# Bias generator without GpSimd and with 19 evict buffers; second unit's loads behind the bias writes

## The chip, the cores and the metric

The kernel runs on one core of one Trainium2 chip. The metric is the device time of one execution in microseconds, median over several runs; lower is better. Times in the profile are in microseconds from the start of the span.

## What is computed

Attention with a learned relative bias, followed by a two-matrix feed-forward block; 4 batches, 8 heads, sequence 576, head width 64, feed-forward 512 to 2048 to 512:

```python
scores = scale * np.matmul(q, k.transpose(0, 1, 3, 2))
psi_rel = np.log1p(np.abs(pos[:, None] - pos[None, :]))
psi_i = np.log1p(np.maximum(pos[:, None], 1.0))
h = np.maximum((psi_rel / psi_i)[..., None] @ w1 + b1, 0.0)   # 32 hidden units
scores = scores + (h @ w2).transpose(2, 0, 1)[None]           # bias of 8 heads
attn = softmax(scores)
x = np.matmul(attn, v)          # to (tokens, 512)
h = x @ w_in
out = np.maximum(0.01 * h, h) @ w_out
```

The bias depends on the position of the row and on the distance alone, and is the same for all four batches.

## The kernel before, in words

The work has three stages on the same engines. The **generator** makes the bias rows and writes them to a scratch buffer in device memory; **attention** works through 16 units (4 pairs of heads by 4 batches) of 9 tiles; then the **feed-forward** block runs in token blocks of 512.

**The generator** takes 36 row groups T of 16 rows each, in the order of the list GEN. For one group the relu rows r (128 partitions: 4 rows by 32 hidden units; up to 576 columns) are made four times: by VectorE (DVE) or GpSimd (POOL) with an add and a max (L111), or by ScalarE (ACT) as a Relu (L109). A planner at L87 to L97 picks the engine: it keeps a running load for each and gives each relu to the one that would be done first. Its costs for a row of w columns are 0.24 + 0.00072 w us on ACT, 0.11 + 0.00056 w on DVE and 0.2 + 0.0044 w on POOL, with 0.84 us on ACT per group for the evictions. Its plan gives 18 relus to ACT, 114 to DVE and 12 to POOL. Rows r come from a ring of 13 buffers. TensorE multiplies the four with w2 (L122), ACT copies the result from PSUM in two pieces into an evict buffer e (L129, L130; a ring of 5), and SyncE's queue (SP) writes e to the scratch buffer scr (L141, 295.5 KB). `gen_tick(g)` writes this down in the order: relus of group g+1 (and of g+3 on POOL), matmuls of g, eviction of g-1. `load_bias` loads finished parts of scr into bias tiles, named 0, 1, M, 2, 3, three loads each (two for M); the ticks at which this is done stand in a table in `gen_tick`.

**Attention.** All generator ticks are written ahead of the first attention tile (GEN_AT). A unit u needs its q and k, loaded by `load_unit` (four loads of 288 and 304 KB, L177 and L178) into one of two sets of buffers raw, and v, by `load_v` (three loads). q and k are then split into a rounded part and a rest: `split_hi` is a cast on DVE (L193 for q, L198 for k), `split_lo` a subtraction on POOL (L205 for q, L208 for k, in two pieces). The 9 tiles of a unit are A0 B0 A1 B1 M A2 B2 A3 B3; tile n belongs to unit n // 9. `step(n)` writes the scores of tile n (L231, first with the rounded k, then with its rest), bias and minimum on DVE (L253), the exponential on ACT (L254), then the reciprocals of the tile before, the product with v (PV, L331) where one is due, and the transposes (L291) of tile n-3. The table SPL says behind which tile of a unit the next unit's splits stand; at tile 4 `load_unit(u+2)`, at tile 8 `load_v(u+2)` is written. Bias tiles A2, B2 use part 2, and A3, B3 part 3.

**What sets the order.** Every engine runs its own list in the order in which the code writes it, SP as well: one queue issues all DMAs, and an issue that waits holds back all issues behind it. The 8 DMA semaphores go round, so that an issue also waits for the landing of the one eight places ahead of it.

Attention output goes to tiles xs for the first 512 tokens and to x1 (four tiles of 128 by 1792) for the rest. x1 is empty until the first unit's output.

## Time and profile before

| | us |
|---|---|
| runs | 746.71, 748.47, 748.63 (median 748.47) |
| the profiled execution's own time | 747.11 |
| its span | 745.3 |
| generator: first relu to first L253 of attention | 4.17 to 61.28 |
| unit 0 (tiles 0 to 8) | 61.28 to 72.38 |
| unit 1 (tiles 9 to 17) | 72.38 to 90.60 |
| units 2, 3, 4 | 16.6, 16.5, 16.5 each |
| busy PE, DVE, ACT, POOL | 717.7, 400.0, 367.2, 151.3 |

A tile's start is the start of its L253. Busy PE counts pipelined matmuls whose ends are modelled, so 96% of the span isn't a TensorE at its peak. DVE and POOL are busiest in the generator, whose relus are theirs.

### The profile page before, as it was taken

Reading aid. Unit: us, or ns where it says so; the run is one execution under the profiler, and the core shown is the slowest. Engines: PE = TensorE matmul, PEld = TensorE weight load, DVE = VectorE, ACT = ScalarE, POOL = GpSimd, SP = SyncE. Lnnn points to the kernel's source line nnn. Section 1 sums busy time; section 2 is a strip of 40 time slices with the busy share of each in tenths; the row PEclk is TensorE's granted clock in tenths of the full one; section 3 lists DMA queues with packets and bytes.
Section 4 is the critical chain, followed back from the end, with each engine's and each line's share of the span. In section 5 each row is a group of like instructions: output and inputs, shape, how many; then the busy total and the mean of one; then the engine's idle time right before and its main releaser. Section 6 shows DMA issues by size and latency. Waiting matters only on the chain.

```text
span 745.3 us, 11450 instructions
## 1 busy us (share of the span) xinstructions
PE 717.7 (96%) x4192; PEld 555.9 (75%) x4192; DVE 400.0 (54%) x1011; ACT 367.2 (49%) x797; POOL 151.3 (20%) x179
## 2 busy tenths in 40 slices
PE   6899999999999999998999999999999999999998
PEld 3236787777777777876887888888888888888896
DVE  8998778778788888848999311111211221111211
ACT  4778677876777777774555321222212222112221
POOL 2684444444354444400000000000000000000000
PEclk9999999999999999999999999999999999999999
DMA  9889839733936653102553010000100000000100
GB/s 222 260 241 263 205 86 234 162 83 112 262 88 165 164 165 91 37 22 78 177 172 110 1 56 1 1 0 1 57 0 1 0 27 31 0 1 1 57 1 29
DMA packets 30264, 68.27 MB, mean 92 GB/s; under 512 B 8192, under 2 KB 8320, under 8 KB 30208
## 3 DMA queue, kind: packets, MB, share of 16 engines
q1 hardware_dynamic: 30208, 67.54, 32.9%
q8 instruction: 33, 0.54, 0.3%
q14 instruction: 23, 0.19, 0.1%
HBM read 51.92 MB, written 15.61 MB: 91 GB/s over the span
## 4 chain that ended last, share of the span: by engine, by line
PE 80%; DVE 9%; ACT 6%; DMA 3%; issue 1%; POOL 0%; DVEq 0%; POOLq 0%; ACTq 0%
PE ps_o L435 13%; PE ps_t L435 13%; PE ps_o L331 10%; PE ps_s L461 9%; PE ps_s L462 9%; PE ps_s L463 9%; PE ps_s L231 6%; PE ps_t L291 6%; DVE p L253 3%; ACT p L254 3%; DVE r L111 3%; ACT PT L307 2%; PE ps_t L122 1%; PE ps_o L122 1%; PE ps_s L122 1%
## 5 line engine op out<-in xcount | busy, mean ns | idle before, releaser
L450 DVE TENSOR_TENSOR gl<-g,gh 128x512 fp32r<-128x512 f32 (+1 forms) x80 | 51.0, 638 | 270.5 <-ACT g L444 270.5
L231 PE MATMUL ps_s<-ks,qs 128*128 128x288 f32 x640 | 119.5, 313 | 1.5 <-DVE mx L253 1.5
L254 ACT ACTIVATE p<-p,mx 128x576 f32<-128x576 f32 x128 | 99.5, 777 | 38.3 <-DVE mx L253 21.4
L461 PE MATMUL ps_s<-woh,gh 128*128 128x512 f32 x288 | 113.7, 395 | 1.6 <-ACT g L444 1.6
L462 PE MATMUL ps_s<-wol,gh 128*128 128x512 f32 x288 | 113.9, 395 | 0.0
L463 PE MATMUL ps_s<-woh,gl 128*128 128x512 f32 x288 | 113.0, 392 | 0.5 <-DVE gl L450 0.5
L253 DVE CUSTOM_DVE_ANT_0 p<-ps_s,bias 128x576 f32<-128x576 f32 x128 | 95.0, 752 | 29.8 <-PE ps_s L231 26.8
L231 PEld LDWEIGHTS ps_s<-ks,qs 128*128 128x128 f32 x640 | 89.6, 189 | 2.9 <-DVE mx L253 2.2
L307 ACT COPY PT<-ps_t 128x512 f32<-128x512 f32 x128 | 73.4, 574 | 30.1 <-PE ps_t L291 29.9
L443 ACT ACTIVATE gh<-ps_o 128x512 fp32r<-128x512 f32 (+1 forms) x39 | 21.5, 552 | 127.8 <-PE ps_o L435 127.8
L291 PE MATMUL ps_t<-ident,p 128*128 128x128 f32 x512 | 79.5, 278 | 3.4 <-ACT PT L307 2.5
L443 ACT ACTIVATE gh<-ps_t 128x512 fp32r<-128x512 f32 (+1 forms) x39 | 21.5, 551 | 114.4 <-PE ps_t L435 114.2
L291 PEld LDWEIGHTS ps_t<-ident,p 128*128 128x128 f32 x512 | 58.5, 140 | 21.1 <-ACT PT L307 7.5
L331 PE MATMUL ps_o<-PT,v 128*64 128x288 f32 x512 | 69.2, 412 | 0.4 <-ACT PT L298 0.4
L461 PEld LDWEIGHTS ps_s<-woh,gh 128*128 128x128 f32 x288 | 54.2, 188 | 14.3 <-ACT g L444 2.0
L463 PEld LDWEIGHTS ps_s<-woh,gl 128*128 128x128 f32 x288 | 54.4, 189 | 13.6 <-DVE gl L450 1.3
L462 PEld LDWEIGHTS ps_s<-wol,gh 128*128 128x128 f32 x288 | 54.3, 189 | 11.6
L435 PE MATMUL ps_o<-xh,wil 128*128 128x512 f32 (+1 forms) x156 | 58.5, 375 | 0.0
L435 PE MATMUL ps_o<-xl,wih 128*128 128x512 f32 (+1 forms) x156 | 58.4, 375 | 0.0
L435 PE MATMUL ps_t<-xh,wil 128*128 128x512 f32 (+1 forms) x156 | 58.3, 374 | 0.0
L435 PE MATMUL ps_o<-xh,wih 128*128 128x512 f32 (+1 forms) x156 | 58.2, 373 | 0.0
L435 PE MATMUL ps_t<-xl,wih 128*128 128x512 f32 (+1 forms) x156 | 58.1, 373 | 0.0
(93 smaller groups left out, 1133.2 us busy)
## 6 DMA issues: line engine op xcount, KB each, us to landing
raw<-kt SPq DMA_DIRECT2D x32, 304.0 KB, 7.3
scr<-e SPq DMA_DIRECT2D x32, 295.5 KB, 3.4
raw<-qt SPq DMA_DIRECT2D x32, 288.0 KB, 7.0
raw<-wi SPq DMA_DIRECT2D x16, 512.0 KB, 3.8
raw<-wo SPq DMA_DIRECT2D x16, 512.0 KB, 3.6
bias<-scr SPq DMA_DIRECT2D x16, 288.0 KB, 4.1
out<-x SPq DMA_DIRECT2D x18, 256.0 KB, 2.1
v<-vm SPq DMA_DIRECT2D x16, 256.0 KB, 6.2
```

The costliest lines, as they stand in the source:

```text
L231: nc.tensor.matmul(s_[:, S0 + HS * hh:S0 + HS * hh + HS], qs[:, c0:c0 + 128], ks[:, k0 + HS * hh:k0 + HS * hh + HS], start=(j == 0), stop= ...
L253: nc.vector.tensor_tensor_reduce(out=p, in0=s_[:, S0:S0 + S], in1=bt, scale=-0.125, scalar=3.4e38, op0=ALU.add, op1=ALU.min, accum_out=i)
L254: nc.scalar.activation(out=p, in_=p, func=AF.Exp, bias=i, scale=-1.0, accum_out=sm_t[n][:, col:col + 1])
L291: nc.tensor.transpose(t0[:, 128 * jb:128 * jb + 128], p[:, p0 + 128 * jb:p0 + 128 * jb + 128], ident[:])
L307: nc.scalar.copy(out=PT[u, g][:, 0:8, c].rearrange("p (j h) c -> p j h c", h=2)[:, :, h, :], in_=t0[:].rearrange("p (j c) -> p j c", j=4))
L331: nc.tensor.matmul(o[64 * h:64 * h + 64, 0:HS], l, r, start=(jb == 0), stop=(jb == 4))
L435: nc.tensor.matmul(h_[:, :N], w, x[:, :N], start=(j == 0), stop=(j == len(mms) - 1))
L443: nc.scalar.activation(out=gh[:, :N], in_=h_[:, :N], func=AF.Prelu, alpha=0.01)
L450: nc.vector.tensor_sub(gl[:, :N], g[:, :N], gh[:, :N].bitcast(F32))
L461: nc.tensor.matmul(o, gh[:, c], wt[m][2][:], start=(m == 0), stop=False)
L462: nc.tensor.matmul(o, gh[:, c], wt[m][3][:], start=False, stop=False)
L463: nc.tensor.matmul(o, gl[:, c], wt[m][2][:], start=False, stop=(m == MF - 1))
```

## The change

The evict buffers become 19: seven tiles of their own, and twelve pieces of 591 columns in the four x1 tiles, taken in turn. The planner loses POOL: all relus go to ACT (22) and DVE (122). The ring of rows r shrinks from 13 to 9. The ticks at which bias parts are loaded move, and part 3 leaves the table. `load_unit(1)` and `load_v(1)` move from the start of the program to behind the generator, with the load of bias part 3 between them. A table SPL0 puts unit 1's splits behind tiles 5 to 8 of unit 0 (SPL: tiles 0 to 7), and unit 2's q and k loads are written at tile 8 of unit 0 (tile 4 before).

```diff
@@ -26,6 +26,7 @@
 GEN = [16, 17] + list(range(16)) + [34, 35] + list(range(18, 26)) + list(range(33, 25, -1))
 SPL = {0: [(0, "q")], 1: [(1, "q", 0)], 3: [(1, "q", 1)], 4: [(0, "k")], 5: [(1, "k", 0)], 7: [(1, "k", 1)]}
 GEN_AT = [39] * 9
+SPL0 = {5: [(0, "q")], 6: [(1, "q", 0), (1, "q", 1)], 7: [(0, "k")], 8: [(1, "k", 0), (1, "k", 1)]}
 LAG = 3
 BLK = 512
 BLOCKS = [(BLK * i, min(BLK, NT - BLK * i)) for i in range((NT + BLK - 1) // BLK)]
@@ -65,6 +66,9 @@
     cs = gp.tile([128, S + 214], F32, name="cs")
     bps = gp.tile([128, 144], F32, name="bps")
     warm = gp.tile([128, 1], F32, name="warm")
+    W = S + 15
+    e_b = [gp.tile([128, W], F32, name=f"e{i}")[:] for i in range(7)]
+    e_b += [x1[h][:, W * i:W * i + W] for h in range(HP) for i in range(3)]
     psib, ips, ltw = cs[:, 34:178], cs[:, 178:214], cs[:, 214:214 + S]
     w1c, b1c, w2d = cs[:, 0:1], cs[:, 1:2], cs[:, 2:34]
 
@@ -84,31 +88,29 @@
     def gen_w(T):
         return max(S - 16 * T, 16 * T + 16)
 
-    plan, load = [], {"a": 0.0, "v": 0.0, "p": 15.0}
+    plan, load = [], {"a": 0.0, "v": 0.0}
     for T in GEN:
         w = gen_w(T)
         load["a"] += 0.84
-        cost = {"a": 0.24 + 0.00072 * w, "v": 0.11 + 0.00056 * w, "p": 0.2 + 0.0044 * w}
+        cost = {"a": 0.24 + 0.00072 * w, "v": 0.11 + 0.00056 * w}
         eng = ""
         for _ in range(4):
-            e = min((c for c in cost if c != "p" or "p" not in eng and len(plan) >= 2), key=lambda c: load[c] + cost[c])
+            e = min(cost, key=lambda c: load[c] + cost[c])
             load[e] += cost[e]
             eng += e
-        plan.append("".join(sorted(eng, key="avp".index)))
-
-    def gen_r(g, pool):
+        plan.append("".join(sorted(eng)))
+
+    def gen_r(g):
         T = GEN[g]
         w = gen_w(T)
-        r = gr.setdefault(T, [None] * 4)
+        r = gr[T] = [None] * 4
         for q, c in enumerate(plan[g]):
-            if (c == "p") != pool:
-                continue
             k = 4 * T + q
-            t = gp.tile([128, S], F32, tag="r", name="r", bufs=13)
+            t = gp.tile([128, S], F32, tag="r", name="r", bufs=9)
             if c == "a":
                 nc.scalar.activation(out=t[:, :w], in_=ltw[:, :w], func=AF.Relu, bias=bps[:, k:k + 1])
             else:
-                (nc.gpsimd if pool else nc.vector).tensor_scalar(out=t[:, :w], in0=ltw[:, :w], scalar1=bps[:, k:k + 1], scalar2=0.0, op0=ALU.add, op1=ALU.max)
+                nc.vector.tensor_scalar(out=t[:, :w], in0=ltw[:, :w], scalar1=bps[:, k:k + 1], scalar2=0.0, op0=ALU.add, op1=ALU.max)
             r[q] = t
 
     def gen_mm(T):
@@ -125,8 +127,8 @@
     def gen_ev(T):
         pt, o0 = gps.pop(T)
         R, F = 16 * T + 15, S - 16 * T
-        e = gp.tile([128, S + 15], F32, tag="e", name="e", bufs=5)
-        nc.scalar.activation(out=e[:, R:], in_=pt[:, o0:o0 + F], func=AF.Copy, scale=ips[:, T:T + 1])
+        e = e_b[GEN.index(T) % len(e_b)]
+        nc.scalar.activation(out=e[:, R:W], in_=pt[:, o0:o0 + F], func=AF.Copy, scale=ips[:, T:T + 1])
         nc.scalar.activation(out=e[:, 0:R], in_=pt[:, o0 + R:o0:-1], func=AF.Copy, scale=ips[:, T:T + 1])
         if T < 16:
             c, r0 = str(T // 8), 16 * (T % 8)
@@ -137,19 +139,17 @@
         else:
             c, r0 = "M", 32 + 16 * (T - 34)
         a = r0 * H * PIT + 1
-        dst = scr[c][a:a + 16 * (H * PIT + 1)].rearrange("(i x) -> i x", i=16)[:, 0:H * PIT].rearrange("i (h p) -> i h p", h=H)[:, :, 0:S + 15]
-        nc.sync.dma_start(out=dst, in_=e[:])
+        dst = scr[c][a:a + 16 * (H * PIT + 1)].rearrange("(i x) -> i x", i=16)[:, 0:H * PIT].rearrange("i (h p) -> i h p", h=H)[:, :, 0:W]
+        nc.sync.dma_start(out=dst, in_=e)
 
     def gen_tick(g):
         if g + 1 < 36:
-            gen_r(g + 1, False)
-        if g + 3 < 36:
-            gen_r(g + 3, True)
+            gen_r(g + 1)
         if 0 <= g < 36:
             gen_mm(GEN[g])
         if 0 <= g - 1 < 36:
             gen_ev(GEN[g - 1])
-        for c in {13: "0", 28: "1", 31: "M", 38: "23"}.get(g, ()):
+        for c in {16: "0", 24: "1", 26: "M", 34: "2"}.get(g, ()):
             load_bias(0, c)
 
     bias = {}
@@ -472,9 +472,8 @@
 
     with tc.manual_schedule():
         gen_setup()
-        for u in range(2):
-            load_unit(u)
-            load_v(u)
+        load_unit(0)
+        load_v(0)
         sp_ops = [(u, w, a) for u in range(1) for w, a in (("q", None), ("q", 0), ("q", 1), ("k", None), ("k", 0), ("k", 1))]
         done = -1
         early_ops = []
@@ -487,6 +486,10 @@
                     if done >= 6 and done % 2 == 0 and sp_ops:
                         w = sp_ops.pop(0)
                         split_hi(*w[:2]) if w[2] is None else split_lo(*w)
+                if i == 0:
+                    load_unit(1)
+                    load_bias(0, "3")
+                    load_v(1)
             if n == 8:
                 gen.close()
                 early = ctx.enter_context(tc.tile_pool(name="early", bufs=1, side="right"))
@@ -515,9 +518,9 @@
                     if c:
                         load_bias(u // B + 1, c)
                 if u + 1 < HP * B:
-                    for f, *args in SPL.get(i, ()):
+                    for f, *args in (SPL if u else SPL0).get(i, ()):
                         (split_hi, split_lo)[f](u + 1, *args)
-                if i == 4 and u + 2 < HP * B:
+                if i == (4 if u else 8) and u + 2 < HP * B:
                     load_unit(u + 2)
                 if i == 8 and u + 2 < HP * B:
                     load_v(u + 2)
```

In the rows below, scr_73, 74, 75, 76 are the scratch buffers of parts 0, 1, 2, 3; raw_78 and raw_79 are q and k of units 0 and 2, raw_80 and raw_81 those of unit 1. L141 and L111 of before are L143 and L113 of the changed kernel.

SP's queue where the generator ends, before: the last writes, then the loads of parts 2 and 3, then unit 2's loads.

```order
L141 DMA scr_76<-e 16x8x591 x5
L166 DMA bias<-scr_75 128x576
L167 DMA bias<-scr_75 128x512
L168 DMA bias<-scr_75 128x64
L166 DMA bias<-scr_76 128x576
L167 DMA bias<-scr_76 128x512
L168 DMA bias<-scr_76 128x64
L177 DMA raw_78<-qt 64x1152
```

The same place in the changed kernel.

```order
L166 DMA bias<-scr_75 128x576
L167 DMA bias<-scr_75 128x512
L168 DMA bias<-scr_75 128x64
L143 DMA scr_76<-x_2_71 16x8x591
L143 DMA scr_76<-x_3_72 16x8x591
L177 DMA raw_80<-qt 64x1152
L178 DMA raw_81<-kt 64x1216
L177 DMA raw_80<-qt 64x1152
L178 DMA raw_81<-kt 64x1216
L166 DMA bias<-scr_76 128x576
```

Part 2's loads now stand ahead of the last two writes, and unit 1's four loads, which stood at the start of the program, stand between the last write and part 3.

DVE where attention begins, before: the cast of unit 1's q stands behind the first tile (ISA with p and mx is L253; mx alone is its second half).

```order
L111 TENSOR_SCALAR r<-cs,bps 128x432 x3
L253 ISA p,mx<-ps_s,bias 128x576
L253 ISA mx 128x1
L193 CAST qs_97<-raw_80 128x2x576
L253 ISA p,mx<-ps_s,bias 128x576
```

DVE in the changed kernel, from the reciprocal behind tile 5 to tile 8.

```order
L261 RECIPROCAL sm<-sm 128x1
L193 CAST qs_97<-raw_80 128x2x576
L253 ISA p,mx<-ps_s,bias 128x576
L253 ISA mx 128x1
L313 COPY PT<-ps_o 128x2x256
L253 ISA p,mx<-ps_s,bias 128x576
L253 ISA mx 128x1
L260 TENSOR_SCALAR sm<-sm 128x2
L261 RECIPROCAL sm<-sm 128x2
L301 COPY PT<-ps_o 64x2x32 x4
L198 CAST ks_865<-raw_81 128x1216
L253 ISA p,mx<-ps_s,bias 128x576
```

The q cast now stands between tiles 5 and 6, and the k cast between tiles 7 and 8.

POOL in the generator, before: unit 0's rests (L205, L208) and relus.

```order
L205 TENSOR_TENSOR qs_96<-raw_78,qs_96 64x576 x2
L111 TENSOR_SCALAR r<-cs,bps 128x400
L111 TENSOR_SCALAR r<-cs,bps 128x368
L208 TENSOR_TENSOR ks_253<-raw_79,ks_252 128x576
L111 TENSOR_SCALAR r<-cs,bps 128x336
L208 TENSOR_TENSOR ks_253<-raw_79,ks_252 128x640
L111 TENSOR_SCALAR r<-cs,bps 128x576
```

POOL in the changed kernel, up to unit 1's k (ks_866).

```order
L205 TENSOR_TENSOR qs_96<-raw_78,qs_96 64x576 x2
L208 TENSOR_TENSOR ks_247<-raw_79,ks_246 128x576
L208 TENSOR_TENSOR ks_247<-raw_79,ks_246 128x640
L264 COPY rb<-sm 128x128 x3
L266 COPY pM<-pM 128x64
L205 TENSOR_TENSOR qs_97<-raw_80,qs_97 64x576 x2
L264 COPY rb<-sm 128x128
L208 TENSOR_TENSOR ks_866<-raw_81,ks_865 128x576
```

The relus are gone from POOL, and unit 1's k rest stands directly ahead of its tiles.

## Rows read from the trace of the kernel before

**Rows 1.** The page: the chain that ended last, by engine.

```profile
PE 80%; DVE 9%; ACT 6%; DMA 3%; issue 1%; POOL 0%; DVEq 0%; POOLq 0%; ACTq 0%
```

**Rows 2.** Stretches: us; busy (instructions) of PE, PEld, DVE, ACT, POOL; clock; DMA share; GB/s.

```profile
13.30:20.50 7.20, 4.50 (x20) 0.75 (x16) 7.20 (x14) 1.72 (x5) 3.03 (x2) 0.98 1.03 303
30.00:40.00 10.00, 9.19 (x71) 3.38 (x70) 10.00 (x21) 6.23 (x14) 8.38 (x6) 1.00 0.78 233
50.00:60.50 10.50, 10.50 (x77) 3.64 (x74) 9.56 (x21) 8.33 (x19) 5.17 (x3) 1.00 0.91 276
```

**Rows 3.** Groups by line, 0 to 61 us: busy, mean ns of one, idle before.

```profile
L111 DVE TENSOR_SCALAR r<-cs,bps 128x320 f32<-128x320 f32 (+17 forms) x114 | 53.0, 540 | 1.2 <-PE ps_t L122 0.9 <-PE ps_o L122 0.3
...
L111 POOL TENSOR_SCALAR r<-cs,bps 128x400 f32<-128x400 f32 (+8 forms) x12 | 25.0, 2087 | 10.5 <-PE ps_t L122 6.8 <-PE ps_o L122 2.4 <-PE ps_s L122 1.2
...
L109 ACT ACTIVATE r<-cs,bps 128x304 f32<-128x304 f32 (+10 forms) x18 | 12.2, 683 | 1.7 <-DVE cs L79 1.7
```

**Rows 4.** ACT's waits, 0 to 61 us: total, times, longest.

```profile
ACT e L129 <- DMA scrM<-e: 5.5, 2, 5.1
```

**Rows 5.** Timeline of DVE, merged: start, us from start to end, instruction, count.

```profile
4.17 8.74 DVE L111 TENSOR_SCALAR r<-cs,bps 128x320 f32<-128x320 f32 x23
12.83 0.75 DVE L193 CAST qs<-raw 128x1152 fp32r<-128x1152 f32 x1
...
13.88 3.15 DVE L111 TENSOR_SCALAR r<-cs,bps 128x496 f32<-128x496 f32 x2
...
22.02 1.14 DVE L111 TENSOR_SCALAR r<-cs,bps 128x432 f32<-128x432 f32 x2 [0.90 <-PE ps_t L122]
...
26.84 2.15 DVE L111 TENSOR_SCALAR r<-cs,bps 128x384 f32<-128x384 f32 x2
...
59.13 0.43 DVE L111 TENSOR_SCALAR r<-cs,bps 128x432 f32<-128x432 f32 x1
61.28 0.76 DVE L253 CUSTOM_DVE_ANT_0 p<-ps_s,bias 128x576 f32<-128x576 f32 x1 [1.72 <-PE ps_s L231]
```

**Rows 6.** DMA issues at 1.64, 2.86, 3.50, 61.66, 65.42: size, us to landing.

```profile
raw<-qt SPq DMA_DIRECT2D x1, 288.0 KB, 4.7
...
raw<-qt SPq DMA_DIRECT2D x1, 288.0 KB, 6.1
...
raw<-kt SPq DMA_DIRECT2D x1, 304.0 KB, 6.9
...
scr<-e SPq DMA_DIRECT2D x1, 295.5 KB, 3.6
...
bias<-scr SPq DMA_DIRECT2D x1, 288.0 KB, 3.5
```

**Rows 7.** Timeline of SP's issues, merged.

```profile
51.13 0.59 SPq L166 DMA_DIRECT2D bias<-scr  x1
...
53.07 1.18 SPq L141 DMA_DIRECT2D scr<-e  x2
...
57.13 5.07 SPq L141 DMA_DIRECT2D scr<-e  x5
```

**Rows 8.** Timeline around tile 9, of DVE, POOL and PE.

```profile
69.78 0.75 DVE L253 CUSTOM_DVE_ANT_0 p<-ps_s,bias 128x576 f32<-128x576 f32 x1
...
70.74 0.93 DVE L301 COPY PT<-ps_o 64x64 f32<-64x64 f32 x4
...
72.38 0.75 DVE L253 CUSTOM_DVE_ANT_0 p<-ps_s,bias 128x576 f32<-128x576 f32 x1
...
76.05 0.76 DVE L253 CUSTOM_DVE_ANT_0 p<-ps_s,bias 128x576 f32<-128x576 f32 x1 [0.25 <-PE ps_s L231]
...
69.01 1.42 POOL L208 TENSOR_TENSOR ks<-raw,ks 128x576 fp32r<-128x576 f32 x1
...
71.33 0.77 PE L231 MATMUL ps_s<-ks,qs 128*128 128x288 f32 x4
...
72.03 2.16 PE L331 MATMUL ps_o<-PT,v 128*64 128x288 f32 x16
```

**Rows 9.** Stretches as in rows 2, around the generator's wait.

```profile
18.00:20.00 2.00, 0.50 (x3) 0.00 (x0) 2.00 (x7) 1.37 (x3) 0.00 (x0) 1.00 1.02 373
20.00:24.00 4.00, 3.79 (x24) 0.73 (x24) 2.77 (x8) 3.61 (x10) 1.68 (x1) 0.57 0.76 228
```

## Prediction

> **What bounds the kernel now.** I read the chain first, then the stretches, then the single instructions where they leave a question. The chain gives PE 80% [rows 1], but from unit 2 on the units take 16.5 us each on TensorE (the table of the starts), and the change touches nothing there. What it can move is the time up to the second unit, so the question is when tile 9 starts its products. In the generator the stretches show DVE busy for all of 13.3 to 20.5 and 30 to 40, and for 9.56 of the last 10.5 us, while ACT stands at 1.72, 6.23 and 8.33 and the DMA engines are not full behind 30 us (0.78, 0.91) [rows 2]. Of 57 us DVE's relus waited 1.2 [rows 3]. The generator is as long as DVE's relus. This also says what the wait in the plainest view is worth: ACT stood 5.5 us for an evict buffer [rows 4], but DVE worked on all the while [rows 2].
>
> **DVE's time, taken apart.** It goes from 4.17 to the end of the last relu at 59.13 + 0.43 = 59.56 [rows 5]: 55.4 us. While POOL does nothing, 23 relus take 12.83 - 4.17 = 8.66 us, the next one starting before the last has quite ended [rows 5]; the planner's own cost (0.11 us + 0.00056 us a column) gives 8.64 for these 23. By that cost the 114 relus are 40.6 us. Two casts of unit 0 add 2 x 0.7 [rows 5], and the waits 1.2 [rows 3]. The four subtractions of unit 0 on POOL stop DVE: two relus of 496 columns took 3.15 us instead of 0.85 [rows 5], which is 1.15 a piece, so 4 x 1.15 = 4.6. That leaves 55.4 - 40.6 - 1.4 - 1.2 - 4.6 = 7.6 us, and what is left to cause it are POOL's 12 relus: beside one, two relus of 432 took 1.14 us where 0.78 is due, and of two of 384 the first is 0.3 longer as well [rows 5].
>
> **No relu on POOL.** Minus 7.6 and, since ACT no longer stands, minus most of the 1.2. DVE gets 8 more relus with 3200 columns in all: 8 x 0.11 + 3200 x 0.00056 = 2.7 us. ACT gets 4 more of 0.68 [rows 3], and has the room. The ring of 9 lets DVE run one group ahead instead of two; in the first ten microseconds its rows come free about as fast as it wants them, and I allow 0.6. The generator becomes 7.6 + 1.2 - 2.7 - 0.6 = 5.5 us shorter. It is no less than 3.9 (if DVE still waits 1.2 and the ring costs 1.0), no more than 6.1 (the ring costs nothing). Tile 0 then starts at 61.28 - 5.5 = 55.8; I call this moment Z, in both kernels (61.28 before).
>
> On the lock between the two engines the rows and a page part ways. Beside a POOL relu of 1.7 us a DVE relu is held for 0.35 [rows 5], not for the whole of it. The Trainium skill (SBUF — State Buffer, Who interferes with whom) has the loser of the shared port pair fully blocked for the other's whole instruction; with 25.0 us of POOL relus the gain would by that be near 22 us. The rows, in which DVE lost 7.6, decide.
>
> **19 evict buffers.** They take away the 5.5 us of [rows 4], which is hidden behind DVE, so nothing beyond the 1.2 above. They cost nothing: the writes land 3.6 us after issue [rows 6], far ahead of a ring of 19.
>
> **Loads behind the writes.** At the start this frees DMA time that nobody waits for any more. At the end it makes a chain that wasn't there. Before, the last of the 36 writes was issued just after Z, at the end of the five issues from 57.13 [rows 7]. Now part 2's three loads go in ahead of the last two writes, and on SP such three take 53.07 - 51.13 = 1.9 us [rows 7]. The third last write is issued between Z-2.3 (the last group's four relus take DVE longer than three did) and Z-1.6, so the last one goes at Z+0.9 to Z+1.6 and unit 1's four loads follow at some 0.65 us each. The second q load is issued at about Z+3.1 and, as the second one of unit 0, lands 6.1 us on [rows 6]: Z+9.2. The second k load lands at Z+10.6 (6.9 us [rows 6]). Part 3 must wait for the last write (3.6 us [rows 6]), which is over by then, and comes out of the same engines behind k: Z+11.6, 1 us of transfer further (288 KB at the 303 GB/s of [rows 2]).
>
> DVE's list: tile 5 is done near Z+6 (an estimate: tile 7 came at 69.78 - 61.28 = Z+8.5 [rows 8]); then the q cast stands first and waits until Z+9.2, a wait of some 3 us, with tiles 6, 7 and 8 queued behind it, and ACT and PE behind these. The cast (0.7), tile 6 (0.7) and a copy (0.7) take it to Z+11.3; tile 7 needs part 3: Z+11.6. From tile 7 to the end of the four small copies is 70.74 + 0.93 - 69.78 = 1.9 us [rows 8], then the k cast 0.8: Z+14.3. POOL's first k rest follows (1.42 [rows 8], with 0.2 to start): Z+15.9. Tile 9's second half of products (0.4 of 0.77 [rows 8]) ends at Z+16.3, and there tile 9 starts. Before it started at 72.38, Z+11.1 [rows 8]. This is 5.2 us late. Bounds: 3.6, if unit 1's loads run at the pace of the faster rows and part 3 is there in time; 6.8, if the writes go 0.7 later and part 3 takes another 0.9.
>
> Nothing gives it back. From tile 9 on PE has its full list: its products, PV from 72.03 on and transposes, and tile 10 follows 3.7 us later at 76.05 [rows 8]; its 18.2 us in unit 1 stay what they are. Unit 2's loads, now behind unit 1's v (1 us) and at 1.3 us each, have brought q by about Z+17.5, when tile 10 is due at Z+20: hidden, with some 2 us to spare.
>
> **The clock.** Between tile 8's products at about Z+10.5 and tile 9's at Z+15.9 PE has one tile's products and one group of transposes. The trace has such a place: PE was busy for 0.50 us of 18 to 20, and then ran 20 to 24 at a granted clock of 0.57, that is mostly at the lower of its two levels (1.2 of 2.4 GHz) [rows 9]. 4 us x 0.43 = 1.7 us of full-speed time were lost there. In the generator DVE hid most of that; behind tile 9 PE is the bound and hides nothing. Part of such a spell may fall into the gap itself, so I take 1.2, between 0 and 1.7.
> The Trainium skill (TensorE: Matmul & The Clock Gate, What's actually happening) has the lower level as the idle state, released by activity; by that rule the wait in unit 0 is paid once more after it ends, and [rows 9] agree.
>
> **The sum.** -5.5 + 5.2 + 1.2 = +0.9 us. Against the profiled execution (747.11, of which the span is 745.3) that is 748.0; that execution lies 1.4 below the median of the runs, which is what I forecast against: 748.47 + 0.9 = 749.4. The bounds, taken not all at once, give -1.5 to +3.3, so 747.0 to 751.8. A measurement of this kernel can tell about 0.3% from no change, 2.2 us: 746.2 to 750.7.
>
> **Rivals.**
> *The loads come sooner.* With 3.6 in place of 5.2 and a clock that stays up the sum is -5.5 + 3.6 = -1.9, and -2.5 at the longest gain of the generator: 746.0 to 746.6, faster. For it: at the start the four loads shared the engines with the tables and with v behind them. Against it: there the first and the second q landed at 1.64 + 4.7 = 6.3 and 2.86 + 6.1 = 9.0, with one k between [rows 6]: 1.3 us a load, one behind the other, and that is transfer, not company. Chance 0.17.
> *TensorE stays slow for longer.* One mechanism, behind tile 9: if PE drops in the gap and, with products that come one at a time, drops again, it loses 2 x 1.7. Then -5.5 + 5.2 + 3.4 = +3.1: 751.6, slower. It decides from 2.5 us of lost full-speed time on. For it: PE is nearly empty from Z+7 to Z+16, longer than in [rows 9]. Against it: PV and transposes follow without a break. Chance 0.18.
> *The generator is not shortened as much.* If ACT's four relus or the ring of 9 hold DVE, the gain falls to its lower bound: -3.9 + 5.2 + 1.2 = +2.5, 751.0, slower. For it: ACT is busy for 8.33 of the last 10.5 us [rows 2] and must do the same in a shorter stretch. Against it: it stays under DVE, and behind its wait it has nothing to catch up. Chance 0.10.
> *The forecast*, 749.4 with 747.0 to 751.8: chance 0.55.
>
> **How the numbers follow.** Faster by over 0.3%: the first rival, mostly, and a little of the forecast's lower end, 0.17. Slower: the second and third and the upper end of the forecast, 0.30. Between, 0.53. The range holds 8 in 10: up to 752.0, past both slower rivals' numbers, and down to 746.0, the fast rival's lower one.
>
> **What would show it.** Generator: no stretched relu on DVE, its last relu near 54.1 and tile 0 near 55.8; ACT without a wait for a write. Unit 0: DVE waits about 3 us for raw q ahead of the cast behind tile 5; tile 9 at Z+16, near 72.1; a granted clock under 1 in the stretch around it; from tile 10 on the same steps as before. I am wrong if tile 9 starts at Z+13 or sooner (the chain through cast and rest is not what I think), or if DVE's last relu is later than 56.

## The result and the profile after

The changed kernel takes **752.23 us** (751.03 to 754.64, five runs) against 748.47 (746.29 to 748.63): a ratio of 1.0058, 95% interval 1.0033 to 1.0083. It is slower by 3.8 us. The forecast was +0.9 (749.4), and the range ended at 752.0.

| start of a tile, us | before | after | after, second execution |
|---|---|---|---|
| tile 0 (Z) | 61.28 | 56.07 | 55.61 |
| tile 7 | Z + 8.50 | Z + 14.53 | Z + 13.56 |
| tile 9 | Z + 11.10 | Z + 19.66 | Z + 19.60 |
| tile 10 behind tile 9 | 3.67 | 5.16 | 6.32 |
| tile 18 (unit 2) | 90.60 | 95.46 | 96.09 |

The second execution is that of the same kernel in the last group of experiments. Of after's profiled execution 2.4 us more than before's lie in unit 8 (20.3 against 17.9 us), where DVE waits for raw q in all of these kernels; it is 17.8 in the second execution, so that part isn't the change's.

So the generator became 5.2 us shorter, the way from tile 0 to tile 9 became 8.6 longer, and 1.5 (2.7) went between tiles 9 and 10. From tile 10 to tile 18 the pace is that of before: 14.57 us against 14.55. The sum is -5.2 + 8.6 + 1.5 = +4.9 in the first execution, -5.7 + 8.5 + 2.7 = +5.5 in the second.

**The generator** did what was forecast. The stretches of after (columns as in [rows 2]):

```profile
13.30:20.50 7.20, 6.16 (x35) 1.56 (x29) 7.20 (x14) 4.39 (x11) 3.04 (x2) 1.00 0.60 173
30.00:40.00 10.00, 10.00 (x89) 4.81 (x86) 10.00 (x32) 9.96 (x24) 0.00 (x0) 1.00 0.82 253
50.00:56.00 6.00, 6.00 (x38) 2.69 (x36) 4.35 (x12) 5.27 (x13) 0.00 (x0) 1.00 0.95 306
```

Between 30 and 40 us DVE now does 32 instructions where it did 21, and POOL none. DVE is still full, and in this stretch ACT is full beside it (9.96 of 10.00 us, 6.23 before). The groups of after, up to 56.5 us, beside [rows 3]:

```profile
L113 DVE TENSOR_SCALAR r<-cs,bps 128x304 f32<-128x304 f32 (+17 forms) x122 | 48.6, 478 | 0.3 <-PE ps_s L124 0.3
...
L111 ACT ACTIVATE r<-cs,bps 128x576 f32<-128x576 f32 (+15 forms) x22 | 14.9, 682 | 1.8 <-DVE cs L83 1.8
```

122 relus take less of DVE (48.6 us) than 114 did (53.0), and they wait 0.3 instead of 1.2. ACT's wait of 5.5 us for an evict buffer is gone.

**Unit 0** is where the time went. DVE in after:

```profile
61.09 0.76 DVE L253 CUSTOM_DVE_ANT_0 p<-ps_s,bias 128x576 f32<-128x576 f32 x1
...
67.57 0.76 DVE L193 CAST qs<-raw 128x1152 fp32r<-128x1152 f32 x1 [5.39 <-DMA raw<-qt]
...
70.60 0.76 DVE L253 CUSTOM_DVE_ANT_0 p<-ps_s,bias 128x576 f32<-128x576 f32 x1 [0.99 <-DMA bias<-scr]
...
72.51 0.79 DVE L198 CAST ks<-raw 128x1216 fp32r<-128x1216 f32 x1
73.33 0.76 DVE L253 CUSTOM_DVE_ANT_0 p<-ps_s,bias 128x576 f32<-128x576 f32 x1
...
75.73 0.76 DVE L253 CUSTOM_DVE_ANT_0 p<-ps_s,bias 128x576 f32<-128x576 f32 x1 [1.63 <-PE ps_s L231]
...
79.24 0.76 DVE L193 CAST qs<-raw 128x1152 fp32r<-128x1152 f32 x1 [2.46 <-DMA raw<-qt]
80.89 0.76 DVE L253 CUSTOM_DVE_ANT_0 p<-ps_s,bias 128x576 f32<-128x576 f32 x1 [0.90 <-PE ps_s L231]
```

Read it from the top: tile 5, then 5.4 us of waiting for raw q (3 were forecast), the q cast, tile 7 held by bias part 3, the k cast, tile 8, and tile 9 held by its products. The last two lines are unit 2's q cast, which waits for its load, and tile 10, which starts when TensorE has made its products. The DMAs on which this rests, as SP issued them (timeline of SP, merged), and their time from issue to landing:

```profile
54.82 0.71 SPq L166 DMA_DIRECT2D bias<-scr  x1
...
57.10 1.17 SPq L143 DMA_DIRECT2D scr<-x  x2
58.32 0.60 SPq L177 DMA_DIRECT2D raw<-qt  x1
58.97 1.17 SPq L178 DMA_DIRECT2D raw<-kt  x1
60.19 0.60 SPq L177 DMA_DIRECT2D raw<-qt  x1
60.83 0.59 SPq L178 DMA_DIRECT2D raw<-kt  x1
63.44 0.33 SPq L166 DMA_DIRECT2D bias<-scr  x1
```

The issues at 57.73, 60.19, 60.83 and 63.44, size and us to landing, beside [rows 6]:

```profile
scr<-x SPq DMA_DIRECT2D x1, 295.5 KB, 5.6
...
raw<-qt SPq DMA_DIRECT2D x1, 288.0 KB, 7.3
...
raw<-kt SPq DMA_DIRECT2D x1, 304.0 KB, 8.8
...
bias<-scr SPq DMA_DIRECT2D x1, 288.0 KB, 7.0
```

The last write took 5.6 us where 3.6 was taken, the second q 7.3 for 6.1, the second k 8.8 for 6.9, part 3 7.0 for 3.5. Part 3 could not be issued before the last write had landed, and SP stood still for it from 61.42 to 63.44. TensorE meanwhile, in stretches of after:

```profile
60.00:64.00 4.00, 3.91 (x31) 3.36 (x29) 1.99 (x8) 3.51 (x9) 0.77 (x3) 1.00 1.02 259
64.00:68.00 4.00, 0.22 (x3) 0.00 (x0) 0.43 (x1) 0.00 (x0) 0.00 (x0) 1.00 1.03 223
68.00:72.00 4.00, 2.24 (x10) 2.09 (x10) 2.96 (x10) 1.88 (x4) 2.97 (x3) 0.50 0.99 219
72.00:76.00 4.00, 2.21 (x8) 1.30 (x8) 2.28 (x7) 2.20 (x7) 2.72 (x3) 0.50 1.01 191
76.00:80.00 4.00, 4.00 (x25) 2.12 (x22) 1.50 (x5) 0.87 (x2) 0.58 (x2) 0.72 1.02 266
```

PE did 0.22 us of work between 64 and 68, and then ran at the lower of its two levels (0.50, that is 1.2 GHz) until behind tile 9; the 16 products of PV there took 3.42 us where they took 2.16 [rows 8]:

```profile
75.62 3.42 PE L331 MATMUL ps_o<-PT,v 128*64 128x288 f32 x16
```

### The profile page after: what moved, and what is told of

Read it like the earlier page. It is cut to its first block, busy times and chain, and to the rows that moved or that the text cites. A ratio compares the mean times of both kernels' runs of the same rounds, so it can differ in the third digit from the quotient of the medians.

```text
span 752.7 us, 11440 instructions
## 1 busy us (share of the span) xinstructions
PE 719.1 (96%) x4192; PEld 561.2 (75%) x4192; DVE 396.2 (53%) x1019; ACT 369.3 (49%) x801; POOL 126.0 (17%) x167
## 4 chain that ended last, share of the span: by engine, by line
PE 74%; DVE 16%; ACT 5%; DMA 3%; issue 1%; POOL 0%; SPq 0%; DVEq 0%; POOLq 0%
PE ps_o L435 11%; PE ps_o L331 11%; PE ps_t L435 11%; PE ps_s L462 8%; PE ps_s L461 8%; PE ps_s L463 8%; PE ps_s L231 6%; PE ps_t L291 5%; DVE p L253 3%; ACT p L254 3%; DVE r L113 2%; ACT PT L307 2%; DVE tmp L405 2%; DVE tmp L407 2%; PE ps_o L124 2%; PE ps_t L124 2%
## 5 line engine op out<-in xcount | busy, mean ns | idle before, releaser
L231 PE MATMUL ps_s<-ks,qs 128*128 128x288 f32 x640 | 121.7, 317 | 3.6 <-DVE mx L253 1.8
L254 ACT ACTIVATE p<-p,mx 128x576 f32<-128x576 f32 x128 | 99.4, 776 | 47.1 <-DVE mx L253 27.9
L253 DVE CUSTOM_DVE_ANT_0 p<-ps_s,bias 128x576 f32<-128x576 f32 x128 | 95.2, 752 | 33.8 <-PE ps_s L231 31.9
L231 PEld LDWEIGHTS ps_s<-ks,qs 128*128 128x128 f32 x640 | 91.4, 193 | 5.6 <-DVE mx L253 2.3
L331 PE MATMUL ps_o<-PT,v 128*64 128x288 f32 x512 | 71.0, 421 | 0.5 <-ACT PT L298 0.5
L462 PEld LDWEIGHTS ps_s<-wol,gh 128*128 128x128 f32 x288 | 54.4, 189 | 11.6
```

The costliest lines, as they stand in the source:

```text
L231: nc.tensor.matmul(s_[:, S0 + HS * hh:S0 + HS * hh + HS], qs[:, c0:c0 + 128], ks[:, k0 + HS * hh:k0 + HS * hh + HS], start=(j == 0), stop= ...
L253: nc.vector.tensor_tensor_reduce(out=p, in0=s_[:, S0:S0 + S], in1=bt, scale=-0.125, scalar=3.4e38, op0=ALU.add, op1=ALU.min, accum_out=i)
L254: nc.scalar.activation(out=p, in_=p, func=AF.Exp, bias=i, scale=-1.0, accum_out=sm_t[n][:, col:col + 1])
L331: nc.tensor.matmul(o[64 * h:64 * h + 64, 0:HS], l, r, start=(jb == 0), stop=(jb == 4))
L462: nc.tensor.matmul(o, gh[:, c], wt[m][3][:], start=False, stop=False)
```

## The experiments

Eleven runs were made: ten edited kernels, each starting from before or after, and the changed kernel once more. The places in time are of each one's profiled execution (tile 9 is counted from tile 0, tile 10 from tile 9, tile 18 against before's 90.60), and the ratio is to the runs of before that it shares (medians 749.08, 748.25 and 748.49 in the three groups).

| kernel | tile 0 | tile 9 | tile 10 | tile 18 | median us | ratio, 95% |
|---|---|---|---|---|---|---|
| before | 61.28 | 11.10 | 3.67 | 0 | 748.47 | |
| after | 56.07 | 19.66 | 5.16 | +4.9 | 752.23 | 1.0058 [1.0033, 1.0083] |
| after again | 55.61 | 19.60 | 6.32 | +5.5 | 752.25 | 1.0057 [1.0033, 1.0081] |
| relus only | 57.37 | 11.09 | 3.67 | -3.9 | 745.30 | 0.9957 [0.9939, 0.9976] |
| buffers only | 61.25 | 11.10 | 3.67 | 0.0 | 746.94 | 0.9966 [0.9942, 0.9990] |
| loads at start | 55.77 | 13.96 | 5.60 | -0.7 | 747.42 | 0.9978 [0.9954, 1.0002] |
| loads at start, early splits | 55.70 | 11.39 | 3.55 | -5.4 | 743.36 | 0.9934 [0.9908, 0.9960] |
| late splits only | 60.54 | 15.04 | 6.34 | +5.9 | 752.66 | 1.0056 [1.0031, 1.0081] |
| after with POOL's relus | 60.42 | 18.55 | 6.39 | +9.3 | 757.02 | 1.0120 [1.0088, 1.0153] |
| k cast early | 55.87 | 17.71 | 5.96 | +3.5 | 750.09 | 1.0010 [0.9978, 1.0041] |
| loads on ACT's queue | 55.75 | 20.16 | 5.60 | +5.5 | 754.56 | 1.0078 [1.0055, 1.0100] |
| PE kept busy | 55.95 | 19.37 | 5.16 | +4.4 | 750.72 | 1.0027 [1.0004, 1.0051] |
| loads in mid-generator, early splits | 55.71 | 11.54 | 3.86 | -4.9 | 743.06 | 0.9933 [0.9910, 0.9955] |

What tile 18 has lost or gained in the trace is found again in the medians within 2.1 us; the trace is of one execution, and the runs of a kernel spread over 3 to 9 us.

### Relus only

Before, with POOL taken out of the planner; ring of 13, five evict buffers, loads and splits as before.

```diff
-            e = min((c for c in cost if c != "p" or "p" not in eng and len(plan) >= 2), key=lambda c: load[c] + cost[c])
+            e = min((c for c in cost if c != "p"), key=lambda c: load[c] + cost[c])
```

> The kernel before with one part of the change alone: no relu on GpSimd; 5 evict buffers, ring of 13, loads at the start. Theory: DVE's relus are the generator's length, so nearly the whole gain is here: tile 0 at 56 to 57, 743.5 to 744.5 us. Rival (the wait for an evict buffer sets the length): tile 0 at 59.5 or later, 747 or more.

Tile 0 comes 3.9 us sooner and everything behind it keeps its distance. The relus of DVE in this kernel, 0 to 61 us:

```profile
L111 DVE TENSOR_SCALAR r<-cs,bps 128x304 f32<-128x304 f32 (+17 forms) x122 | 48.6, 476 | 1.5 <-PE ps_o L122 1.5
```

Eight more relus and 4.4 us less of DVE: POOL's relus did stretch DVE's, by 4.4 + 2.7 = 7.1 us where 7.6 was forecast (2.7 is the forecast's price of the eight). The gain is under what was expected, at tile 0 (57.37) and in time (745.30); ACT still stands 5.9 us for an evict buffer in this kernel, and the relus wait 1.5 us for products.

### Buffers only

Before, with 17 evict buffers (five of their own and the twelve in x1).

```diff
...
-        e = gp.tile([128, S + 15], F32, tag="e", name="e", bufs=5)
...
+        e = e_b[GEN.index(T) % len(e_b)]
...
```

> The kernel before with one part of the change alone: 17 evict buffers (5 of their own, 12 in the empty output tiles). Theory: ACT's wait of 5.5 us is gone and DVE's 1.2 us at most: tile 0 at 60.1 to 61.3, 747.3 to 748.5 us. Rival (that wait sets the length): tile 0 at 56 to 58, 743.5 to 745.5.

The relus of DVE and POOL in it, 0 to 61 us (L114 here is L111 of before), and the start of the first ones:

```profile
L114 DVE TENSOR_SCALAR r<-cs,bps 128x320 f32<-128x320 f32 (+17 forms) x114 | 53.2, 544 | 0.0
...
L114 POOL TENSOR_SCALAR r<-cs,bps 128x400 f32<-128x400 f32 (+8 forms) x12 | 28.2, 2359 | 6.3 <-PE ps_t L125 3.8 <-PE ps_o L125 2.2 <-PE ps_s L125 0.2
...
4.84 0.35 DVE L82 TENSOR_SCALAR cs<-cs 128x256 f32<-128x256 f32 x1 [0.77 <-DMA cs<-cst]
5.11 8.74 DVE L114 TENSOR_SCALAR r<-cs,bps 128x320 f32<-128x320 f32 x23
```

DVE's wait is gone (0.0 for 1.2), and yet tile 0 stands where it stood, 61.25. The reason is at the start: in this execution a table landed late, and the first relu starts at 5.11 instead of 4.17. From the first relu to tile 0 it is 56.14 us, 57.11 before: 1.0 shorter. Not all of that need be the buffers': before's profiled execution has a stretch at the lower clock at 20 us [rows 9], in which DVE waited for products, and the run with late splits only, whose generator is that of before, ran the same stretch at full clock and took 56.18. A generator's length is known to about 1 us from one execution. From the first relu, POOL's relus taken out alone give 4.1 us, and all the kernels without them and with 19 buffers 5.3 to 5.7; these have the ring of 9 and the other ticks too, which were not run by themselves. The median is 2.1 us under before's; where that comes from is open.

### Loads at the start

After, with unit 1's loads back at the start of the program; late splits kept.

```diff
-        load_unit(0)
-        load_v(0)
+        for u in range(2):
+            load_unit(u)
+            load_v(u)
...
-                    load_unit(1)
                     load_bias(0, "3")
-                    load_v(1)
```

> The changed kernel with unit 1's q, k and v loaded at the start again; relus, 19 evict buffers, part 3's load and the splits behind tiles 5 to 8 stay. Theory (the relus shorten the generator, the loads behind the writes cost more than that): tile 0 at 56 to 57, tile 9 some 11 to 12 us behind it, the clock full around tile 9, 744 us. Rival (the generator is shorter because the start of the DMA queue is free): tile 0 at 59 or later, 746.5 or more.

Tile 9 comes at 13.96, not at 11 to 12. The wait for raw q is gone, so 5.7 of the 8.6 us are the loads' landing. The rest stayed although q and k had long been there, and so did the clock loss. DVE's tiles 7, 9 and 10:

```profile
64.94 0.76 DVE L253 CUSTOM_DVE_ANT_0 p<-ps_s,bias 128x576 f32<-128x576 f32 x1 [1.14 <-PE ps_s L231]
...
66.83 0.79 DVE L198 CAST ks<-raw 128x1216 fp32r<-128x1216 f32 x1
...
69.73 0.76 DVE L253 CUSTOM_DVE_ANT_0 p<-ps_s,bias 128x576 f32<-128x576 f32 x1 [1.32 <-PE ps_s L231]
...
75.33 0.76 DVE L253 CUSTOM_DVE_ANT_0 p<-ps_s,bias 128x576 f32<-128x576 f32 x1 [3.78 <-PE ps_s L231]
```

A second cause was therefore wanted: the places of the splits.

### Late splits only, and early splits

Late splits only is before with the change's table of places for unit 1's casts and subtractions and nothing else; its counterpart, early splits, is the kernel above (loads at the start) with these put back to their places of before, and unit 2's loads to tile 4.

```diff
+SPL0 = {5: [(0, "q")], 6: [(1, "q", 0), (1, "q", 1)], 7: [(0, "k")], 8: [(1, "k", 0), (1, "k", 1)]}
...
-                    for f, *args in SPL.get(i, ()):
+                    for f, *args in (SPL if u else SPL0).get(i, ()):
```

> The kernel before with one edit: unit 1's casts and subtractions in the late places of the change (two subtractions together behind the tile after the cast). Loads, generator and buffers as before. Theory: tile 0 unchanged at 61.3, tile 9 at 13 to 14 us behind it instead of 11.1, since the k cast stands behind tile 7 and the two k subtractions behind tile 8; then a spell of lower clock behind tile 9 and tile 10 5.0 to 5.6 us later instead of 3.7; time 751.5 to 753.5. Rival (with everything landed early the late casts are hidden): tile 9 at 11.1 to 11.5, time 748 to 749.

> The changed kernel with unit 1's loads at the start of the program and with unit 1's casts and subtractions in the places that they have in the kernel before (tiles 0 to 7); what is left of the change is the generator without GpSimd's relus, the 19 buffers and the ticks of the bias loads. Theory (the late casts and subtractions cost about 2.9 us up to tile 9 and 1.9 us of lower clock behind it, even where the raw parts are there): tile 0 at 55.8, tile 9 at 11.1 to 11.8 us behind it (the last bias part still lands near 9 us behind tile 0 and may hold tile 7 by 0.7), no spell of lower clock behind tile 9, unit 1 18.2 us, time 743 to 744. Rival (what tile 9 waits for in the run with the loads at the start is the late bias part, not the late casts): tile 9 at 13 to 14 us behind tile 0, a spell of lower clock, time 746.5 to 748.

Both settle it. With early splits tile 9 comes at 11.39, there is no lower clock, and the kernel is 4.9 us faster than before (0.2 of the 11.39 is a wait for part 3). With late splits alone tile 9 comes at 15.04, tile 10 at 6.34 (14 and 5.6 were the most expected), and a kernel whose unit 1 has landed long before is as slow as the change. Its tile 0 comes at 60.54, 0.7 sooner than before's, with the same generator: DVE waited 0.5 us for products in it instead of 1.2. DVE and POOL in it (its lines are one further down than before's, so L254 is L253 and L261 is L260):

```profile
69.56 0.76 DVE L254 CUSTOM_DVE_ANT_0 p<-ps_s,bias 128x576 f32<-128x576 f32 x1 [0.21 <-DMA bias<-scr]
70.25 0.08 DVE L254 DVE_READ_ACCUMULATOR2_ANT mx<- 128x1 f32 x1
70.25 1.06 DVE L261 TENSOR_SCALAR sm<-sm 128x2 f32<-128x2 f32 x1
...
72.37 0.79 DVE L199 CAST ks<-raw 128x1216 fp32r<-128x1216 f32 x1
73.19 0.76 DVE L254 CUSTOM_DVE_ANT_0 p<-ps_s,bias 128x576 f32<-128x576 f32 x1
...
75.58 0.76 DVE L254 CUSTOM_DVE_ANT_0 p<-ps_s,bias 128x576 f32<-128x576 f32 x1 [1.63 <-PE ps_s L232]
81.92 0.76 DVE L254 CUSTOM_DVE_ANT_0 p<-ps_s,bias 128x576 f32<-128x576 f32 x1 [4.61 <-PE ps_s L232]
...
68.50 2.79 POOL L206 TENSOR_TENSOR qs<-raw,qs 64x576 fp32r<-64x576 f32 x2
```

From tile 7 to tile 9 it is 6.02 us, 2.60 before. The k cast ahead of tile 8 is 0.8 of the difference, the wait of tile 9's products for cast and subtraction 1.7, and 0.9 is a step that nobody would cost at anything: L261 adds a constant to two columns, 0.16 us in before's trace, 1.06 here. It ends at 71.31, as POOL's pair of q subtractions ends at 68.50 + 2.79 = 71.29. The Trainium skill (SBUF — State Buffer, Who interferes with whom) says that an operation of this form can need the port pair that the two engines share, and that the one that comes second is then fully blocked for the other's whole instruction; here the trace agrees. In after the same pair ends as late tile 7 does (71.25), so it costs nothing there; in the second execution of after tile 7 comes 1 us sooner, and L260 takes 1.08 us: part 3's landing and POOL's pair cover each other.

### After with POOL's relus

After with the planner, the ring of 13 and the POOL relus of before, 17 buffers: a long generator with late loads.

```diff
-    plan, load = [], {"a": 0.0, "v": 0.0}
+    plan, load = [], {"a": 0.0, "v": 0.0, "p": 15.0}
...
-            gen_r(g + 1)
+            gen_r(g + 1, False)
+        if g + 3 < 36:
+            gen_r(g + 3, True)
```

> The changed kernel with the relus on GpSimd again (12, the planner and the ring of 13 of before, 17 evict buffers): the generator is long, the loads stand behind the writes. Theory (the loads land late because a shorter generator crowds the same writes and bias loads together): tile 0 at 60 to 61.3, the last write lands 3.6 to 4.0 after its issue, unit 1's second q some 9.5 us behind tile 0 and not 11.4, tile 9 at 16.5 behind it and not 19.7, and the same clock loss of 1.5: about 754.8 us. Rival (the loads are as late for a cause of their own): tile 9 at 19.5 behind tile 0, about 757.5.

It was made to see whether the loads land late because the shorter generator packs the same writes closer. In the last four microseconds ahead of tile 0 (56 to 60) the DMA engines are 0.74 busy here; in after they are at 0.95 from 50 to 56. The second q is again issued 4.1 us behind tile 0; it lands 6.3 us later instead of 7.3, at Z+10.5, and tile 9 is 1.1 sooner (18.55). That is nearer the rival's 19.5 than the theory's 16.5, and so is the time (757.02). Nor is the 1 us shown to be the packing's: the second execution of after has 6.2 us, and in the four executions with a short generator and the loads in this place on SP the second q lands at Z+10.4 to Z+11.5. Most of the lateness comes with the place of the loads.

### Loads on ACT's queue

After, with unit 1's four loads issued by ACT behind its last eviction.

```diff
...
-                    load_unit(1)
+                    load_unit(1, nc.scalar)
```

> The changed kernel with unit 1's four loads issued from ScalarE's DMA queue behind its last eviction, in place of SyncE's queue behind the last write; everything else as in the change, the late casts too. Theory (what makes the loads land late is that the 16 DMA engines are full, 0.95 to 1.0 from 40 us on, whichever queue asks): the second q lands no sooner than 10 us behind tile 0 (11.4 in the change), tile 9 18 to 20 us behind it, time 750.5 to 752.5. Rival (the one queue in order is the cause: the second q is issued 4.1 us behind tile 0 and waits its turn behind writes and part 2): issued by 2 us, landed by 8 to 9 us behind tile 0, tile 9 at 15.5 to 17, time 748 to 750.

The second q is issued 2 us sooner (2.05 behind tile 0) and lands 9.7 behind it instead of 11.4: between the two expectations, and the time is worse than either. What it met on the way:

```profile
raw<-qt ACTq DMA_DIRECT2D x1, 288.0 KB, 7.7
...
61.34 0.78 ACT L254 ACTIVATE p<-p,mx 128x576 f32<-128x576 f32 x1 [5.42 <-DMA raw<-kt]
```

It takes 7.7 us to land, and the last of the 36 writes, on SP's queue, goes from 5.6 to 8.2: the two queues share one set of full engines (0.94 to 1.03 between 56 and 64 us). Then ACT stands for 5.4 us at the issues of the second q and k, at 57.80 and 60.82 (the k's just as the first q has landed, 60.80), with the exponentials of tiles 0 to 2 queued behind them, and tile 3 starts at Z+7.6 instead of Z+2.8. The Trainium skill (DMA: Bandwidth & Descriptors, Issuing engines are not separate DMA queues) says that DMAs of all engines end up on the same 16 engines and that spreading them saves issuing time alone; the two landings agree. The theory that full engines set the landing stands, except that 1.7 us of the second q's lateness (11.4 to 9.7) go with SP's order.

### k cast early

After, with the k cast behind tile 6 and the k subtractions behind tile 7.

```diff
-SPL0 = {5: [(0, "q")], 6: [(1, "q", 0), (1, "q", 1)], 7: [(0, "k")], 8: [(1, "k", 0), (1, "k", 1)]}
+SPL0 = {5: [(0, "q")], 6: [(1, "q", 0), (1, "q", 1), (0, "k")], 7: [(1, "k", 0), (1, "k", 1)]}
```

> The changed kernel with unit 1's k cast behind tile 6 instead of tile 7 and its two k subtractions behind tile 7 instead of tile 8; loads as in the change. Theory (of the change's loss at tile 9, landing and late places add up; in the change k lands 13.6 us behind tile 0 and the cast starts at 16.4): the cast starts as k lands, tile 7 stays at 14.4 to 15.2, tile 9 at 17.2 to 18.1 instead of 19.7, time 1.5 to 2.5 us under the changed kernel. Rival (the cast ahead of tile 7 holds tiles 7 and 8 as much as it gains): tile 9 at 19 to 20, same time.

As the theory had it: tile 9 at 17.71, 2 us sooner, and the median 2.2 us under the second execution's. Part of it may be luck in the landing (the second k lands at Z+11.8 here, Z+12.9 and Z+13.6 in after's two executions, and tile 7, expected at 14.4 or later, comes at 13.37). From tile 7 to tile 9, behind the landing, it is 4.3 us, 5.1 and 6.0 in after's two: that much is the place of the cast. The lower clock stays, and tile 10 takes 5.96.

### PE kept busy

After, with tile 7's products made eight times over and tile 8's three times, into the same place.

```diff
...
-            qk_mm(n)
+            qk_mm(n, {7: 8, 8: 3}.get(n, 1))
```

> The changed kernel with TensorE's products of tile 7 repeated eight times and those of tile 8 three times (same result, more work in the gap ahead of tile 9). Theory (the lower clock behind tile 9, 1.5 us of it between tiles 9 and 10, follows TensorE's idle time ahead of it): granted clock back to 1.0 at tile 9 and tile 10 3.7 to 4.2 us behind tile 9 instead of 5.2, tile 9 itself at 19 to 20 us behind tile 0; time 750.5 to 751.5. Rival (idle time is not what lowers it, or products at the lower clock fill the stretch by themselves): tile 10 5.2 us or more behind tile 9, time 752 to 754.

The time came out as the theory had it, but not by its mechanism. The clock is 1.00 from 64 to 72 us, where it was 0.50 from 68 on, so work in that stretch does keep it up; yet PE still waits 1.1 and 0.9 us ahead of tile 9's two halves, the level falls at 74.4, and PV takes 3.42 us exactly as in after:

```profile
72.00:76.00 4.00, 2.07 (x8) 1.33 (x10) 2.31 (x5) 1.34 (x3) 2.91 (x2) 0.80 1.01 215
76.00:80.00 4.00, 4.00 (x26) 2.30 (x23) 1.04 (x5) 1.13 (x3) 2.12 (x2) 0.78 1.04 358
...
75.22 3.42 PE L332 MATMUL ps_o<-PT,v 128*64 128x288 f32 x16
```

Tile 10 is 5.16 behind tile 9, the rival's number. Up to tile 18 the trace gives 0.3 us back (39.08 us from tile 0, 39.39 in after); the 1.5 in the median aren't explained by it.

### After again

> The changed kernel once more, unedited, since its profiled run was the longest of its five and 2.4 us of that lie in unit 8. Expected: tile 0 at 55.9 to 56.2, tile 9 at 19 to 20 us behind it, tile 10 5.0 to 5.3 behind tile 9, unit 8 anywhere from 17.4 to 18.9 us instead of 20.3, time 751 to 752.5. If unit 8 is again above 20 us, the wait in it belongs to the change and the cost has a second place.

Tile 9 and the time are those of after, unit 8 is 17.8 us, and the clock loss is larger than expected:

```profile
75.21 0.76 DVE L253 CUSTOM_DVE_ANT_0 p<-ps_s,bias 128x576 f32<-128x576 f32 x1 [1.64 <-PE ps_s L231]
81.53 0.76 DVE L253 CUSTOM_DVE_ANT_0 p<-ps_s,bias 128x576 f32<-128x576 f32 x1 [4.58 <-PE ps_s L231]
...
76.00:80.00 4.00, 4.00 (x18) 1.63 (x14) 0.92 (x3) 0.87 (x2) 2.12 (x2) 0.50 1.04 370
```

The lower level lasts through all of 76 to 80 here, through part of it (0.72) in after: 2.7 us instead of 1.5. It varies from one execution to the next of the same kernel.

### Loads in the middle of the generator

After, with unit 1's loads one per tick from tick 6 on, early splits, and unit 2's loads at tile 4.

```diff
...
+        mid = unit_loads(1)
...
                     done += 1
+                    if done >= 6 and mid:
+                        f, *args = mid.pop(0)
+                        f(*args)
...
```

> The changed kernel with unit 1's loads in the middle of the generator, one per tick from tick 6 on, where the DMA engines are 0.60 to 0.65 busy, and its casts and subtractions in the places of the kernel before. Theory (only the late landing and the late casts cost): tile 0 at 55.5 to 56.2, tile 9 at 11.1 to 11.8 us behind it, no lower clock at 20 us and none behind tile 9, time 742.5 to 744, the fastest of all. Rival (the DMA engines have no room for the loads beside writes and bias loads): the last bias part, or a buffer, comes 1 to 2 us later, tile 9 at 12.5 to 13.5 behind tile 0, time 745 to 746.

743.06, the same as with the loads at the start (743.36). The stretch from 13.3 to 20.5 us, whose DMA share was 0.60 in after, takes them:

```profile
13.30:20.50 7.20, 6.16 (x30) 1.52 (x26) 7.20 (x14) 4.20 (x10) 3.04 (x2) 1.00 0.91 273
```

These two beat both kernels: 5 us under before (ratio 0.9933, 0.9910 to 0.9955), 9 under the change. They keep the change's generator and buffers and leave out its moved loads and splits.

## Why the prediction was wrong, step by step

**Right.** That DVE's relus are the length of the generator, and that POOL's stretch them: -5.5 forecast, -5.2 and -5.7 measured, with the last relu ending at 54.35 (54.1 forecast); both are against one execution of before, whose generator took 0.9 us less in another (late splits only). That ACT's wait of [rows 4] was mostly hidden: of its 5.5 us the buffers alone give back 1.0 at most. The order of events in unit 0 (q cast, part 3 at tile 7, k cast, POOL, tile 9), the lower clock behind the gap, and that nothing is given back from tile 10 on (14.57 against 14.55 us). Unit 2's q was hidden, but barely: it was forecast for Z+17.5 and landed at Z+23.1 (Z+20.2 in the second execution); in the first DVE waited 2.5 us for it, and tile 10 still waited longer, for its products.

**Wrong: the term "Loads behind the writes", +5.2 forecast, +8.6 measured.** By its own steps in the two executions of after:

| step | forecast | after | second execution |
|---|---|---|---|
| last write issued | Z+0.9 to 1.6 | Z+1.7 | Z+2.6 |
| second q issued | Z+3.1 | Z+4.1 | Z+5.3 |
| its landing | 6.1 on: Z+9.2 | 7.3 on: Z+11.4 | 6.2 on: Z+11.5 |
| second k lands | Z+10.6 | Z+13.6 | Z+12.9 |
| tile 7, with part 3 | Z+11.6 | Z+14.5 | Z+13.6 |
| tile 7 to tile 9 | 4.7 | 5.1 | 6.0 |
| tile 9 | Z+16.3 | Z+19.7 | Z+19.6 |

2.9 of the 3.4 us were lost by tile 7 in the first execution, 2.0 of 3.3 in the second; there tile 7 comes sooner, and L260's 1.08 us behind it take most of the rest. The step that failed is the landing of unit 1's loads: the second q came at Z+11.4 and Z+11.5, 2.2 and 2.3 us later than forecast. The lateness has two parts, a longer flight and a later issue, in different shares in the two executions.

*The flight.* I took flight times from [rows 6], of q and k at the start of the program with nothing ahead of them but the tables and each other, and for the last write the 3.6 us of before, where only writes stood ahead of it; now part 2 does too. Behind the generator the engines were 0.95 to 1.0 busy, and everything there stood in line: 1.2 us more in the first execution, 0.1 in the second.

*The issue.* Part 2's loads held SP for 2.3 us (54.82 to 57.10; 2.7 in the second execution) and not 1.9, and the first k for 1.2 and not 0.65, so that the second q was issued 1.0 and 2.2 us later than forecast. Why these issues took longer is open.

The sentence that part 3's write "is over by then" was the second slip: it took 5.6 us, and SP stood for it; tile 7 waited 1.0 us for part 3 in the first execution, not at all in the second. The bound of 6.8 allowed for 0.7 and 0.9 of this, not for 2.9. Whether the shorter generator itself adds to the lateness is not shown: with POOL's relus back the second q landed at Z+10.5, with a short generator at Z+10.4 to Z+11.5.

The bookkeeping also hid the second half of the term. The forecast's way from tile 7 to tile 9, 4.7 us, is 2.1 longer than before's 2.60, and that is the price of the late places alone. It was in the sum, but inside a chain that was told as the loads' price; so the text didn't say that the late splits cost 2.6 to 3.9 us at tile 9 (13.96 against 11.39, 15.04 against 11.10), and the clock besides, with q and k there (tile 10 at 5.60 against 3.55, and 6.34 against 3.67).

**The clock** was forecast at +1.2 with an end of 1.7, and it took 1.5 and 2.7. The rival of a longer spell put its point at 2.5 us of lost time: the second execution went that way, the first didn't. Every kernel whose PE waits ahead of tile 9 for the late cast and subtraction has the loss there (tile 10 at 5.16 to 6.39, eight executions), every other hasn't (3.55 to 3.86). What in the gap decides between 1.5 and 2.7 is open; keeping PE busy in its first part alone didn't remove it.

**The rivals.** *Loads come sooner* fell: they came later. *Generator not shortened as much* fell. *TensorE slow for longer* gave 751.6, near the time measured, but by a larger clock term and a chain of 5.2; it was the chain.

## What to carry to other kernels

A flight time is that of the queue it was measured in: for a transfer that is moved behind others, count the kilobytes that stand ahead of it on the DMA engines at that moment and divide by the rate of that stretch, and look at whether an issue behind it must wait for one of those to land. Here that would not have been enough: the second q with the four transfers ahead of it is 1.5 MB, by an estimate 6.1 us at the 259 and 223 GB/s of its stretches, and it took 7.3 and 6.2. Price the issues as well: here they made the second q 1.0 and 2.2 us late before it was under way. Where work that feeds the next stage is moved to just ahead of it, cost the move twice, with the data late and with the data there: here the late places (with unit 2's loads behind them) took back 4.7 of the 5.4 us that the generator had gained at tile 18. And a stretch that is made shorter raises the DMA rate inside it by itself (from 276 GB/s over 50 to 60.5 us before to 306 over 50 to 56 in after); look at its share before something else is put behind it.

## What the runs showed of the hardware

- Behind the generator a transfer of 288 to 304 KB took 5.6 to 8.8 us to land, 3.5 to 6.9 in the rows of before; the DMA share was 0.95 to 1.03 all the while, but the rate fell from 306 GB/s (50 to 56 us, writes and loads of bias rows) to 223 (64 to 68 us, when q and k landed). A full share is no fixed rate.
- An operation of two columns on DVE, 0.16 us, took 1.06 and 1.08 beside a subtraction on POOL, and ended within 0.1 us of it.
- An engine whose queue is given loads waits in its own list where an issue has to wait: ACT stood 5.4 us, with three exponentials behind it.
- The same kernel lost 1.5 us to the lower clock in one execution and 2.7 in another.
